# Position bias by w2 times the relu layer in fp32, laid out by DMA, in place of threshold masks

## The chip, the cores and the metric

The kernel runs on one core of one Trainium2 chip. The metric is the device time of one execution in microseconds, the median of three timed runs. The engines are named as the profile names them: PE (TensorE, matrix products) and PEld (its weight loads), DVE (VectorE), ACT (ScalarE), POOL (GpSimd), SP (SyncE, which here only issues DMAs).

## The reference

Attention with a learned position bias, then a gated MLP, then a token and channel mixing stage. All of it is fp32. The part that changes is the bias:

```python
pos = np.arange(S)                       # S = 576
rel = (pos[:, None] - pos[None, :]).astype(np.float32)
psi_rel = np.log1p(np.abs(rel))
psi_i = np.log1p(np.maximum(pos[:, None].astype(np.float32), 1.0))
x = (psi_rel / psi_i)[..., None]
h = np.maximum(x @ w1 + b1, 0.0)         # w1 (1, 32), b1 (32)
bias = h @ w2                            # w2 (32, 8): one bias per head
scores = scores + bias.transpose(2, 0, 1)[None, :, :, :]
...
attn = np.exp(scores)
attn = attn / (np.sum(attn, axis=-1, keepdims=True) + 1e-09)
```

So each pair of a query row i and a key column j has one scalar x, 32 relu units on it, and 8 head biases. The bias is the same for the 4 batches. Shapes: batch 4, 8 heads, 576 positions, head size 64; the later stages are 512 wide (the MLP 1024).

## The kernel before

The bias is made once, at the start, and lies in SBUF for all batches: four tiles `bias0` to `bias3` of 128 query rows x 8 heads x 576 columns, and `biasr`, which holds the last 64 rows with even heads in the lower 64 partitions and odd heads in the upper. Then come 144 attention tiles of 128 rows x 576 columns (16 pairs of heads, 9 tiles each): products `s` from `kh`, `kl` and `qs`; DVE adds the bias and takes the row's extreme in one custom instruction (`e<-s,bias`, which gives the row extreme `m`); ACT takes the exponential; `p` is split into two fp16 halves; a DMA transposes it (`pT`), and PE multiplies with `v` (`px`). Between attention pairs run the MLP of the batch before (`vp`, `up`, `sp`) and, at the start, the unpacking of `w_in` (`rawwi`, `cvawi`). After attention come the output product `op`, the unpacking of further weights (`cvaw_tok`, `wr_w_tok` and the like) and the mixing stages (`tp`, `yp`, `cp`).

The bias before (function `bias_gen`, lines 662 to 773) uses that a relu unit is linear in x on one side of a threshold. 45 units of work, each 128 rows x 64 columns, run through four engines. DVE compares a table of distances `ds` with thresholds `th` and writes a 0/1 mask `mk` of 128 x 2048 fp16, in which the partitions are 4 columns x 32 hidden units. PE takes 16 slices of the mask as weights and multiplies each with `ch` and `cl` (w2 times w1 and w2 times b1 in two fp16 parts), 32 products a unit, into `pb`. This gives slope and offset for each head. ACT copies the offset to `cc`, DVE multiplies the slope with the x table `xt` to `bt` (in every sixth unit ACT copies and POOL multiplies instead), and POOL adds the two into the bias tile. `pb` has two buffers of its own and, for every third unit, one of the score buffers (`PBN`, `pbt`); `mk` has three buffers. Beside it, twelve loads `vr` of v and their squares on ACT give the scale of v.

The order of all instructions is not the order of the code. `Rec` records every operation with a key, and `plan` (line 382) runs a list scheduler over them: each operation has a cost from `cost` (line 549), the key is shifted by a number for each name (`SHIFT`), and where an operation may go to one of several engines (`any`, line 300), a number for each name and engine (`BIAS`) weighs the choice. The instructions are then issued in that order on each engine; each engine and each DMA queue works its own in order. All of them carry the helper's line in the profile (L366), so groups are told apart by tile names.

The last part of a unit, after the products, is:

```python
nc.scalar.activation(cc, pv[:, H:], AF.Copy, scale=ci8)
...
nc.vector.tensor_tensor(tmp[r, :nh], pv[r, hs], xs[r].bc(1, nh), op=ALU.mult)
self.tt(("gpsimd",), dv, tmp[r, :nh], cc[r, hs], ALU.add)
```

Of the kernel before, what the change touches and what calls it, by code (L numbers as in the profile page):

```python
# [218 lines left out]
}  # L219
SHIFT = {  # L220
    "aw": -17.4929, "bias": 41.9326, "biasr": -68.9186, "bsg": 97.9286, "bt": -5.7555, "c": -279.9533, "ca": 22.1144,
    "cc": 295.8081, "ch": -73.6056, "ci": 36.2217, "cl": 17.4554, "cp": 15.2786, "cvaw_ch": 69.6045,
    "cvaw_out": -194.7794, "cvaw_theta": 8.5825, "cvaw_tok": -207.7246, "cvawi": -0.5182, "cvsw_ch": 161.0008,
    "cvsw_out": 0.6877, "cvsw_theta": -99.9127, "cvsw_tok": 85.3798, "cvswi": 2.3671, "ds": 47.8704, "e": -0.6132,
    "eps": 169.8, "fa_c": -50.561, "fa_v": 185.4902, "fa_wi": -255.4938, "fa_ws": 58.9062, "fb_c": -277.5272,
    "fb_v": 19.4726, "fb_wi": -86.0368, "fb_ws": 64.453, "fc_c": 164.9752, "fc_v": 223.2589, "fc_wi": 7.0491,
    "fc_ws": 28.1163, "fd_c": -314.7184, "fd_v": -444.6712, "fd_wi": -6.1476, "fd_ws": -20.5742, "fs_c": 244.1602,
    "fs_v": -273.363, "fs_wi": -108.0749, "fs_ws": -26.7084, "g": 98.9891, "gg": 3.2775, "ghs": -197.3784,
    "gr": 14.9268, "gsc": -167.0231, "gts": 44.5279, "gtu": -15.6392, "gtv": -6.823, "halfpi": 90.4852, "i": 26.7498,
# [351 lines left out]
class K:  # L581
# [74 lines left out]

    def pbt(self, u, n=0):
        if PBN[n % len(PBN)]:
            return self.ps_s.tile([P, 2, 512], F32, tag="sc", bufs=2, name=f"pb{u}")
        return self.ps_b.tile([P, 2, 512], F32, tag="pb", bufs=2, name=f"pb{u}")  # L660

    def bias_gen(self):
# [15 lines left out]
        sg2 = st.tile([P, 1], F32, name="sg2")
        aw = st.tile([P, 1], F32, name="aw")
        rt = st.tile([P, 1], F32, name="rt")  # L680
        nc.vector.tensor_scalar(sg, w1, 0.0, 2.0, op0=ALU.is_ge, op1=ALU.mult)
        nc.vector.tensor_scalar(sg2, sg, -1.0, None, op0=ALU.add)
        nc.vector.tensor_scalar(aw, w1, sg2, 1e-30, op0=ALU.mult, op1=ALU.max)
        nc.vector.reciprocal(rt, aw)
        nc.vector.tensor_scalar(rt, rt, b1, sg2, op0=ALU.mult, op1=ALU.mult)
        nc.vector.tensor_scalar(rt, rt, -1.0, 1e6, op0=ALU.mult, op1=ALU.min)
        nc.vector.tensor_scalar(rt, rt, -1e6, None, op0=ALU.max)
        y, y2 = prow, st.tile([P, S], F32, name="y2")
        nc.vector.tensor_scalar(y, prow, rt, 20.0, op0=ALU.mult, op1=ALU.min)
        nc.vector.tensor_scalar(y, y, -40.0, None, op0=ALU.max)  # L690
        nc.scalar.activation(y2, y, AF.Exp)
        nc.vector.tensor_scalar(y, y2, 700.0, -1.5, op0=ALU.min, op1=ALU.add)
        nc.vector.tensor_scalar(y2, y, MAGIC, MAGIC, op0=ALU.add, op1=ALU.subtract)
        th = st.tile([P, S], F16, name="th")
        self.th = nc.vector.tensor_scalar(th, y2, 0.5, sg2, op0=ALU.add, op1=ALU.mult)
        nc.vector.tensor_scalar(ds, ds, sg2, None, op0=ALU.mult)
        c32 = st.tile([P, 2, H, 4], F32, name="c32")
        nc.vector.memset(c32, 0.0)
        for g in range(4):
            r = slice(32 * g, 32 * g + 32)  # L700
            nc.vector.tensor_scalar(c32[r, 0, :, g], w2[r], w1[r], None, op0=ALU.mult)
            nc.vector.tensor_scalar(c32[r, 1, :, g], w2[r], b1[r], None, op0=ALU.mult)
        c32f = c32.rearrange("p a h g -> p (a h g)")
        junk = self.bsg[:, :64]
        for i in range(2):
            nc.scalar.activation(junk, c32f, AF.Square, accum_out=self.ss_c[:, i:i + 1])
# [634 lines left out]
```

## Time and profile before

| what | us |
|---|---|
| time, median of 3 runs | 963.27 |
| the runs | 957.67, 963.27, 965.01 |
| the profiled execution: span from the first to the last instruction | 948.8 |
| busy PE / PEld | 736.5 / 598.6 |
| busy DVE | 747.9 |
| busy ACT | 562.5 |
| busy POOL | 441.5 |

For the profiled execution the page gives its span and no other time; the median of the runs lies 14.5 us above this span. Busy time is the union of an engine's instructions and says nothing of who waits for whom. That is read from the waits (who waited for whom, and how long) and from the chain that ended last. A mean in nanoseconds is the length of one instruction; instructions of one engine can overlap a little, so a count times a mean can be more than the busy time.

### The profile page before, as it was taken

To read this page: it belongs to the slowest core of one execution; us is meant where nothing else is said; L and a number is where in the kernel's file an instruction comes from. 1 tells how busy PE (TensorE), PEld (TensorE's weight loads), DVE (VectorE), ACT (ScalarE), POOL (GpSimd) and SP (SyncE) were. 2 spreads that over 40 slices of the span, in tenths; PEclk is the share of its full clock that TensorE was granted. 3 is DMA by queue.
4 is the path that set the end of the run, shared out by engine and by line. 5 is a ranking of instruction groups with operands and counts; after the bars stand their busy time and mean duration, and the time that the engine had idled before them with its cause. 6 is when DMAs were issued, how large, how long until landed. Compare 5 with 4: busy or idle time off the path is not lost.

```text
span 948.8 us, 19542 instructions
## 1 busy us (share of the span) xinstructions
PE 736.5 (78%) x7322; PEld 598.6 (63%) x7322; DVE 747.9 (79%) x1544; ACT 562.5 (59%) x1144; POOL 441.5 (47%) x373
## 2 busy tenths in 40 slices
PE   4345445665575895979878989899778999999998
PEld 3345444554464664655555655576757899999998
DVE  8798978889987788998999796898998884372622
ACT  7413148868776777877877684765555673261510
POOL 1667784545545464564556563145643532041310
PEclk9667876756669888899979999999988999999999
DMA  7300019889899999999989995645541110010001
GB/s 250 104 1 2 1 30 255 166 167 217 152 197 207 204 194 183 192 225 218 190 186 199 231 179 154 208 138 176 182 134 48 34 52 34 1 51 1 26 26 50
DMA packets 223871, 124.79 MB, mean 132 GB/s; under 512 B 195616, under 2 KB 195744, under 8 KB 223776
## 3 DMA queue, kind: packets, MB, share of 16 engines
q1 hardware_dynamic: 214560, 101.88, 50.0%
q10 hardware_dynamic: 9216, 21.67, 7.9%
q8 instruction: 57, 0.93, 0.4%
q14 instruction: 38, 0.31, 0.1%
HBM read 62.17 MB, written 14.16 MB: 80 GB/s over the span
## 4 chain that ended last, share of the span: by engine, by line
PE 38%; DVE 28%; DMA 15%; issue 10%; ACT 7%; POOL 1%; SPq 0%; ACTq 0%; DVEq 0%; POOLq 0%
PE yp L366 11%; DMA pT<-p 6%; DVE mk L366 5%; PE cp L366 4%; PE s L366 4%; DVE e L366 4%; PE op L366 3%; PE tp L366 3%; PE pb L366 3%; PE px L366 3%; DMA xp<-x 3%; PE up L366 2%; DVE x L366 2%; DVE cvaw_tok L366 2%; PE sp L366 2%
## 5 line engine op out<-in xcount | busy, mean ns | idle before, releaser
L366 POOL TENSOR_TENSOR p<-e,p 128x576 f16<-128x576 f32 x144 | 194.4, 1358 | 152.7 <-ACT p L366 132.5
L366 PE MATMUL s<-kh,qs 128*128 128x288 f32 (+1 forms) x320 | 94.0, 390 | 63.9 <-DVE m L366 39.6
L366 ACT ACTIVATE e<-e,m 128x576 f32<-128x576 f32 x144 | 110.4, 767 | 42.1 <-DVE m L366 37.7
L366 PE MATMUL px<-v,pT 128*128 128x64 f16 (+1 forms) x2240 | 102.5, 206 | 41.1 <-DMA pT<-p 34.3
L366 PEld LDWEIGHTS <-pT 128*128 128x128 f16 (+1 forms) x2240 | 89.0, 110 | 68.8 <-DMA pT<-p 46.1
L366 PE MATMUL yp<-wk,z 128*128 128x288 f32 x864 | 118.3, 296 | 0.7 <-ACT z L366 0.4
L366 PEld LDWEIGHTS yp<-wk,z 128*128 128x128 f32 x864 | 115.6, 188 | 1.8 <-ACT z L366 0.9
L366 PEld LDWEIGHTS s<-kh,qs 128*128 128x128 f32 (+1 forms) x320 | 59.3, 222 | 85.5 <-DVE m L366 31.7
L366 PE MATMUL pb<-ch,mk 128*128 128x64 f16 x720 | 60.0, 213 | 65.6 <-ACT cc L366 34.4
L366 DVE CUSTOM_DVE_ANT_0 e<-s,bias 128x576 f32<-128x576 f32 x128 | 95.7, 751 | 13.0 <-PE s L366 11.4
L366 ACT ACTIVATE p<-e 128x576 f16<-128x576 f32 x140 | 92.8, 671 | 18.3 <-DMA pT<-p 13.5
L366 PEld LDWEIGHTS <-mk 128*128 128x128 f16 x1440 | 58.4, 111 | 68.0 <-DVE mk L366 54.8
L366 PE MATMUL s<-kl,qs 128*128 128x288 f32 (+1 forms) x320 | 84.9, 362 | 6.4 <-DVE kl L366 6.1
L366 DVE TENSOR_TENSOR mk<-ds,th 128x2048 f16<-128x2048 f16 x45 | 79.5, 1817 | 5.2 <-PE pb L366 5.1
L366 POOL TENSOR_TENSOR bias<-bt,cc 128x512 f32<-128x512 f32 x36 | 62.1, 1745 | 42.8 <-ACT cc L366 24.0
L366 PE MATMUL op<-sp_g,wo 128*128 128x288 f32 x384 | 65.0, 328 | 14.6 <-DVE x L366 9.3
L366 PEld LDWEIGHTS op<-sp_g,wo 128*128 128x128 f32 x384 | 59.1, 212 | 21.3 <-DVE x L366 7.0
L366 PEld LDWEIGHTS s<-kl,qs 128*128 128x128 f32 (+1 forms) x320 | 62.1, 228 | 10.2 <-DVE kl L366 9.2
L366 ACT ACTIVATE cc<-pb,ci 128x512 f32<-128x512 f32 x45 | 29.6, 683 | 62.5 <-DVE bt L366 56.7
L366 PE MATMUL vp<-wi,xT 128*128 128x512 f16 (+1 forms) x240 | 64.2, 395 | 2.2 <-DVE gg L366 2.2
L366 PE MATMUL sp<-ws,n 128*128 128x64 f16 (+1 forms) x384 | 58.7, 293 | 2.8 <-DVE n L366 2.7
L366 DVE TENSOR_TENSOR x<-x,yp 128x576 f32<-128x576 f32 x16 | 12.1, 754 | 61.6 <-PE yp L366 61.6
(228 smaller groups left out, 1651.5 us busy)
## 6 DMA issues: line engine op xcount, KB each, us to landing
raw<-kv ACTq DMA_DIRECT2D x19, 576.0 KB, 4.9
raw<-kv SPq DMA_DIRECT2D x13, 576.0 KB, 4.7
raww_tok<-w_tok SPq DMA_DIRECT2D x18, 288.0 KB, 3.0
vr<-v_all SPq DMA_DIRECT2D x12, 384.0 KB, 3.8
xx<-dx SPq DMA_DIRECT2D x16, 288.0 KB, 3.2
out<-oo SPq DMA_DIRECT2D x16, 288.0 KB, 2.1
xT<-dx SPq DMA_DIRECT2D x7, 576.0 KB, 5.2
gr<-dg SPq DMA_DIRECT2D x14, 288.0 KB, 3.3
```

The lines of the kernel that those rows point to most:

```text
L366: getattr(getattr(self.nc, name), m)(*[res(x) for x in a], **out)
```

## The change

The bias is computed as the reference writes it, in fp32. The partitions are now 4 query rows x 32 hidden units. A table `lt` holds log1p of the distance for a window of 1148 positions, shifted by one from one row of the four to the next, and `sl` holds w1 divided by psi of each row. For four rows at a time one instruction makes the relu layer `hq` (128 x 576): on DVE as max(lt * sl, -b1) with the constant part w2 times b1 added later (`cb`), and, in every third group, on ACT as relu(lt * sl + b1). 144 of these make 36 groups `G` of four. For each group PE multiplies each of the four `hq` with the same small weights `w2f` (128 x 32) in two halves of 288 columns; the four results go to the four 32-partition column groups of one `pb` tile. So a group has 8 products, 288 in all. One instruction (ACT or DVE, as the planner chooses) copies the 128 x 576 result to `bs`, whose partitions are row and head, and a DMA lays it out as 16 rows x 8 heads x 576 in the bias tile. There are no masks, no `xt`, no `bt`, no `cc`, and no POOL work for the bias. `pb` uses its own two buffers alone. `hq` has ten buffers, `bs` three. `cost` prices a product with 32 output partitions at a quarter. The tables of the planner have other numbers throughout, and the DMA issues have numbers of their own in them now.

```diff
 BIAS = {
-    ("gg", "gpsimd"): -9.3524, ("gg", "vector"): -1.4198, ("kh", "scalar"): -12.8265, ("kh", "vector"): 14.8773,
...
+    ("bias", "scalar"): -23.814, ("bias", "sync"): 24.2122, ("biasr", "scalar"): -42.8956,
...
-        return rhs.cols * (4.0 if rhs.t.dt == F32 else 1.068 if rhs.t.dt == F32R else 1.0), rhs.shape[0] / P
+        n = rhs.cols * (4.0 if rhs.t.dt == F32 else 1.068 if rhs.t.dt == F32R else 1.0)
+        return (n / 4 if out.shape[0] == 32 else n), rhs.shape[0] / P
...
-TWO = range(4,45,6)
-PBN = (0,0,1)
+LUTG = 3
...
-        for x, n in ((wb, "wb"), (prow, "prow"), (ds, "dtab")):
-            self.ld(x, d[n], ("sync",))
-        for ib in range(5):
-            nc.key = 1.0 + 15 * ib
-            self.ld(xt[:, ib], d["xtab"][:, ib], ("sync",))
...
+        sl = st.tile([P, S // 4], F32, name="sl")
+        lt = st.tile([P, DW], F32, name="lt")
+        for x, n in ((wb, "wb"), (sl, "rpsi"), (lt, "ltab")):
+            self.ld(x, d[n])
+        nb = st.tile([P, 1], F32, name="nb")
+        nc.vector.tensor_scalar(nb, b1, -1.0, None, op0=ALU.mult)
+        self.th = nc.vector.tensor_scalar(sl, sl, w1, None, op0=ALU.mult)
...
-        for n in range(45):
-            nc.key = 2.0 * n
-            ib, js = divmod(n, 9)
...
-                nc.vector.tensor_tensor(mk, win, th[:, ib * P:(ib + 1) * P].bc(1, 16), op=ALU.is_gt)
...
-            for J in range(16):
-                o = ps[:, J // 8].rearrange("p (r j) -> p r j", j=32)[:, :, J % 8 * 4:J % 8 * 4 + 4]
-                nc.tensor.matmul(o, mk[:, J, :], chv, start=True, stop=False)
-                nc.tensor.matmul(o, mk[:, J, :], clv, start=False, stop=True)
...
+        for g in range(4):
+            nc.tensor.matmul(pc[32 * g:32 * g + 32, 0:1], w2f, bb, start=True, stop=True)
+        nc.vector.tensor_copy(cb, pc[:, 0:1])
...
+        for G in range(36):
+            ps = self.ps_b.tile([P, 2, 512], F32, tag="pb", bufs=2, name=f"pb{G}")
+            hs = []
+            lut = G % LUTG == LUTG - 1
+            for q in range(4):
+                nc.key = 2.5 * G + q * 0.5
+                Q = 4 * G + q
+                h = st.tile([P, S], F32, tag="hq", bufs=10, name=f"hq{Q}")
+                win = lt[:, DOFF - 4 * Q:DOFF - 4 * Q + S]
+                if lut:
+                    nc.scalar.activation(h, win, AF.Relu, scale=sl[:, Q:Q + 1], bias=b1)
+                else:
+                    nc.vector.tensor_scalar(h, win, sl[:, Q:Q + 1], nb, op0=ALU.mult, op1=ALU.max)
+                hs.append(h)
+            for n in range(2):
+                for q in range(4):
+                    nc.tensor.matmul(ps[32 * q:32 * q + 32, n, :SH], w2f, hs[q][:, n * SH:(n + 1) * SH],
+                                     start=True, stop=True)
+            bs = st.tile([P, S], F32, tag="bs", bufs=3, name=f"bs{G}")
+            bv = bs.rearrange("p (n j) -> p n j", n=2)
+            add = zero if lut else cb
+            nc.any(("scalar", "activation", (bv, ps[:, :, :SH], AF.Identity), {"bias": add}),
+                   ("vector", "tensor_scalar", (bv, ps[:, :, :SH], add, None), {"op0": ALU.add}))
+            ib, r0 = divmod(16 * G, P)
...
+                self.ld(self.bm[ib][r0:r0 + 16], bs)
...
+                for e in range(2):
+                    self.ld(self.bm[4][64 * e + r0:64 * e + r0 + 16], bs[e::2])
```

DVE in the middle of the bias, before: masks `mk` (block and unit in the name), and between them the multiplications `bt`.

```order
L366 TENSOR_TENSOR mk1_3_735<-ds_199,th_192 128x2048
L366 TENSOR_TENSOR bt1_2_787<-pb1_2_655,xt_198 128x512 [waits Activation_49]
L366 TENSOR_TENSOR mk1_4_774<-ds_199,th_192 128x2048
L366 TENSOR_TENSOR mk1_7_865<-ds_199,th_192 128x2048 [waits DVE_49,PE_49]
L366 TENSOR_TENSOR mk1_8_902<-ds_199,th_192 128x2048 [waits DVE_49,PE_49]
L366 TENSOR_TENSOR bt1_3_897<-pb1_3_776,xt_198 128x512 [waits Activation_49]
L366 TENSOR_TENSOR bt1_4_908<-pb1_4_790,xt_198 128x512 [waits Pool_49]
L366 TENSOR_TENSOR bt1_5_932<-pb1_5_746,xt_198 128x512 [waits Pool_49]
L366 TENSOR_TENSOR mk2_0_960<-ds_199,th_192 128x2048 [waits DVE_49,PE_49]
L366 TENSOR_TENSOR bt1_6_962<-pb1_6_906,xt_198 128x512 [waits Activation_49]
```

DVE at the fifth to eighth group, after: the relu rows `hq` (numbered by four rows) and the copies `bs` (numbered by group); `kl` belongs to attention.

```order
L379 TENSOR_SCALAR hq16_268<-lt_189,sl_190,nb_188 128x576 [waits DVE_49,PE_49]
L379 TENSOR_SCALAR hq17_276<-lt_189,sl_190,nb_188 128x576 [waits DVE_49,PE_49]
L379 TENSOR_SCALAR bs2_173<-pb2_259,zb_184 128x576 [waits PE_49]
L379 TENSOR_SCALAR bs3_271<-pb3_285,cb_185 128x576 [waits DMAHW3_49,PE_49,Activation_49]
L379 TENSOR_SCALAR hq18_283<-lt_189,sl_190,nb_188 128x576
L379 TENSOR_SCALAR hq19_288<-lt_189,sl_190,nb_188 128x576 [waits Activation_49]
L379 TENSOR_TENSOR kl0_0_111<-raw0_0_118,kh0_0_114 128x576 [waits DMAHW1_49,Activation_49]
L379 TENSOR_SCALAR hq24_312<-lt_189,sl_190,nb_188 128x576 [waits DVE_49]
L379 TENSOR_SCALAR hq27_326<-lt_189,sl_190,nb_188 128x576 [waits DVE_49,PE_49]
L379 TENSOR_SCALAR hq28_337<-lt_189,sl_190,nb_188 128x576 [waits PE_49,Activation_49]
L379 TENSOR_SCALAR hq29_343<-lt_189,sl_190,nb_188 128x576 [waits DVE_49,PE_49]
L379 TENSOR_SCALAR bs5_324<-pb5_318,zb_184 128x576 [waits DMAHW7_49,PE_49]
```

The masks and multiplications are gone; relu rows stand in their place, with a copy `bs` now and then that waits for the products of its group and, from the fourth on, for a DMA as well, because its buffer must have been laid out.

The SP queue around the third to sixth `vr` load, before:

```order
L366 DMA xt_198<-xtab 128x576 [waits DMAHW4_49]
L366 DMA vr2_251<-v_all 128x768 [waits DMAHW6_49,Activation_49]
L366 DMA vr3_265<-v_all 128x768 [waits DMAHW7_49,Activation_49]
L366 DMA rq0_0_117<-qt 64x576 [waits DMAHW0_49]
L366 DMA vr4_333<-v_all 128x768 [waits DMAHW1_49,Activation_49]
L366 DMA vr5_360<-v_all 128x768 [waits DMAHW2_49,Activation_49]
L366 DMA vr6_446<-v_all 128x768 [waits DMAHW3_49,Activation_49]
```

The same place after; `bias0<-bs` is the layout of one group, 16 rows x 8 heads x 576:

```order
L379 DMA vr2_249<-v_all 128x768 [waits DMAHW2_49,Activation_49]
L379 DMA bias0_78<-bs0_171 16x8x576 [waits DMAHW3_49,Activation_49]
L379 DMA vr3_266<-v_all 128x768 [waits DMAHW4_49,Activation_49]
L379 DMA bias0_78<-bs1_172 16x8x576 [waits DMAHW5_49,Activation_49]
L379 DMA vr4_304<-v_all 128x768 [waits DMAHW6_49,Activation_49]
L379 DMA bias0_78<-bs2_173 16x8x576 [waits DMAHW7_49,DVE_49]
L379 DMA bias0_78<-bs3_271 16x8x576 [waits DMAHW0_49,DVE_49]
L379 DMA vr5_347<-v_all 128x768 [waits DMAHW1_49,Activation_49]
L379 DMA bias0_78<-bs4_298 16x8x576 [waits DMAHW2_49,Activation_49]
L379 DMA vr6_367<-v_all 128x768 [waits DMAHW3_49,Activation_49]
L379 DMA bias0_78<-bs5_324 16x8x576 [waits DMAHW4_49,DVE_49]
L379 DMA bias0_78<-bs6_332 16x8x576 [waits DMAHW5_49,Activation_49]
```

Between the loads `vr` stand the layout DMAs, each behind its copy on ACT or DVE, and the loads behind them wait in the queue. Of the 40 layout DMAs (32 of 16x8x576, 8 of 16x4x576) 38 are on SP and two, those of group 34, on ACT.

PE from the fifth group on, after; the column group is the number of `hq` modulo four:

```order
L379 MATMUL pb4_310<-hq16_268,w2s_187 32x288
L379 MATMUL pb4_310<-hq17_276,w2s_187 32x288
L379 MATMUL pb4_310<-hq16_268,w2s_187 32x288
L379 MATMUL pb4_310<-hq17_276,w2s_187 32x288
L379 MATMUL pb5_318<-hq20_291,w2s_187 32x288 x2
L379 MATMUL pb4_310<-hq18_283,w2s_187 32x288 x2
L379 MATMUL pb5_318<-hq21_293,w2s_187 32x288 x2
L379 MATMUL pb4_310<-hq19_288,w2s_187 32x288 x2
L379 MATMUL pb5_318<-hq22_306,w2s_187 32x288 x2
L379 MATMUL pb6_354<-hq24_312,w2s_187 32x288
L379 MATMUL pb6_354<-hq25_314,w2s_187 32x288
L379 MATMUL pb6_354<-hq24_312,w2s_187 32x288
```

The planner has mixed two groups and split some pairs of halves; where a row ends in x2, both halves of one column group follow each other directly.

## Rows read from the trace of the kernel before

**Rows 1.** Windows, four stretches: busy us (instructions), granted clock, DMA share, GB/s.
```profile
10.00:132.00 122.00, 61.09 (x1443) 58.79 (x1444) 107.32 (x94) 44.56 (x76) 79.94 (x52) 0.78 0.15 49
145.00:580.00 435.00, 329.23 (x3509) 238.48 (x3509) 383.17 (x982) 334.21 (x715) 232.31 (x198) 0.83 0.98 194
580.00:750.00 170.00, 148.44 (x987) 111.76 (x985) 144.26 (x267) 98.84 (x203) 75.06 (x72) 0.95 0.45 141
750.00:949.00 199.00, 194.04 (x1363) 186.84 (x1361) 97.98 (x145) 72.18 (x125) 44.91 (x37) 1.00 0.09 31
```

**Rows 2.** Lines, 10 to 132 us: count | busy us, mean ns | idle before, releasers.
```profile
L366 DVE TENSOR_TENSOR mk<-ds,th 128x2048 f16<-128x2048 f16 x45 | 79.5, 1817 | 5.2 <-PE pb L366 5.1
L366 POOL TENSOR_TENSOR bias<-bt,cc 128x512 f32<-128x512 f32 x36 | 62.1, 1745 | 42.8 <-ACT cc L366 24.0 <-DVE bt L366 18.5
L366 PE MATMUL pb<-ch,mk 128*128 128x64 f16 x720 | 60.0, 213 | 65.6 <-ACT cc L366 34.4 <-DVE mk L366 27.4 <-DVE bt L366 3.8
L366 DVE TENSOR_TENSOR bt<-pb,xt 128x512 f32<-128x512 f32 (+1 forms) x42 | 24.6, 608 | 6.3 <-POOL bias L366 3.5 <-ACT cc L366 1.9 <-POOL biasr L366 0.5
```

**Rows 3.** Waits, 10 to 135 us: us in total, times, longest.
```profile
PEld L366 <- DVE mk L366: 54.8, 25, 6.8
```

**Rows 4.** Timeline: start us, us, what; first masks, first attention tile, last bias add.
```profile
10.74 4.63 DVE L366 TENSOR_TENSOR mk<-ds,th 128x2048 f16<-128x2048 f16 x4
...
132.39 0.76 DVE L366 CUSTOM_DVE_ANT_0 e<-s,bias 128x576 f32<-128x576 f32 x1 [0.46 <-PE s L366]
...
137.77 3.77 POOL L366 TENSOR_TENSOR biasr<-bt,cc 64x256 f32<-64x256 f32 x5
```

**Rows 5.** Lines by form, whole span, VectorE: count | busy us, mean ns | idle.
```profile
L366 DVE TENSOR_TENSOR x<-x,yp 128x576 f32<-128x576 f32 x16 | 12.1, 754 | 61.6 <-PE yp L366 61.6
L366 DVE TENSOR_SCALAR prow<-prow,rt 128x576 f32<-128x576 f32 x1 | 0.5, 520 | 0.0
L366 DVE TENSOR_SCALAR y<-prow 128x576 f32<-128x576 f32 x1 | 0.5, 461 | 0.0
```

**Rows 6.** Lines by form, whole span, ScalarE.
```profile
L366 ACT ACTIVATE kh<-raw 128x576 fp32r<-128x576 f32 x32 | 21.5, 673 | 9.7 <-DMA raw<-kv 7.9 <-DMA xp<-x 1.5
L366 ACT ACTIVATE v<-raw,fc_v 128x576 f16<-128x576 f32 x25 | 19.2, 768 | 5.9 <-PE px L366 3.9 <-DMA xp<-x 1.2 <-DVE fc_v L366 0.7
L366 ACT ACTIVATE vr<-vr 128x768 f32<-128x768 f32 x12 | 10.1, 842 | 7.1 <-DMA vr<-v_all 7.0
```

**Rows 7.** Lines by form, whole span, TensorE.
```profile
L366 PE MATMUL yp<-wk,z 128*128 128x288 f32 x864 | 118.3, 296 | 0.7 <-ACT z L366 0.4 <-DVE x L366 0.3
L366 PE MATMUL xp<-ident,x 128*128 128x128 f32 x64 | 10.0, 278 | 3.9 <-DVE rk L366 2.6 <-DVE rw L366 1.3
L366 PE MATMUL pbv<-ssv,ones 128*128 128x2 f32 x2 | 0.4, 262 | 0.4 <-ACT cc L366 0.4
```

**Rows 8.** DMA issues, whole span: KB each, median us to landing.
```profile
rq<-qt SPq DMA_DIRECT2D x20, 144.0 KB, 2.9
wb<-wb SPq DMA_DIRECT2D x1, 5.0 KB, 1.6
```

**Rows 9.** DMA, 0 to 36 us, 40 slices of 0.9 us.
```profile
GB/s 0 1 50 287 396 389 255 300 376 407 404 407 373 411 420 409 329 56 73 273 137 283 126 0 109 300 147 256 89 174 271 156 140 304 201 212 17 0 0 61
```

**Rows 10.** Lines by form, 130 to 949 us: work that changes its engine.
```profile
L366 POOL TENSOR_TENSOR wk<-wr_w_tok,wk 128x576 fp32r<-128x576 f32 x9 | 13.8, 1532 | 9.3 <-ACT wk L366 9.3
L366 POOL TENSOR_TENSOR wr_w_ch<-cvaw_ch,cvsw_ch 128x256 f32<-128x256 f32 x8 | 6.3, 787 | 8.4 <-ACT cvaw_ch L366 7.6 <-ACT cvsw_ch L366 0.9
L366 DVE CAST x<-xf 128x256 f16<-128x256 f32 x7 | 3.5, 498 | 1.2 <-DMA xp<-x 1.1
L366 DVE TENSOR_TENSOR wr_w_theta<-cvaw_theta,cvsw_theta 128x256 f32<-128x256 f32 x2 | 1.8, 908 | 0.0
```

**Rows 11.** Chain that ended last, 150 to 580 us, by line.
```profile
by line: DMA pT<-p 14.2%; PE s L366 9.2%; issue 8.9%; DVE e L366 7.8%; PE px L366 6.1%; DMA xp<-x 5.5%; DMA rawwi<-w_in 3.8%; DVE x L366 3.6%; PE vp L366 2.6%; ACT e L366 2.6%; DVE cvawi L366 2.5%; DMA raw<-kv 2.5%; DVE gtv L366 2.4%; DVE k
```

More of the change, by code (lines that the diff above doesn't have):

```diff
@@ new lines @@
+    ("biasr", "sync"): -32.2509, ("bs", "scalar"): -0.0729, ("bs", "vector"): 0.2057,
+    ("bsg", "scalar"): -10.0381, ("bsg", "sync"): -2.7396, ("g", "scalar"): 10.6989, ("g", "sync"): 44.9021,
+    ("gg", "gpsimd"): 0.6847, ("gg", "scalar"): 4.2248, ("gg", "sync"): -24.7139, ("gg", "vector"): 26.751,
+    ("gr", "scalar"): -0.003, ("gr", "sync"): 40.0654, ("ident", "scalar"): -56.6989,
+    ("ident", "sync"): -54.8165, ("kh", "scalar"): -16.1883, ("kh", "vector"): -12.6842,
[4 rows of a table added]
+    ("qs", "vector"): 0.9315, ("raw", "scalar"): -8.224, ("raw", "sync"): 3.4229, ("raww_ch", "scalar"): 4.5613,
@@ L219 @@
+    ("wr_w_tok", "gpsimd"): 29.6991, ("wr_w_tok", "vector"): 23.1577, ("ws", "scalar"): -11.5258,
+    ("ws", "vector"): 61.9014, ("wsr", "scalar"): 11.35, ("wsr", "vector"): -19.7126,
[4 rows of a table added]
 }
 SHIFT = {
-    "aw": -17.4929, "bias": 41.9326, "biasr": -68.9186, "bsg": 97.9286, "bt": -5.7555, "c": -279.9533, "ca": 22.1144,
-    "cc": 295.8081, "ch": -73.6056, "ci": 36.2217, "cl": 17.4554, "cp": 15.2786, "cvaw_ch": 69.6045,
-    "cvaw_out": -194.7794, "cvaw_theta": 8.5825, "cvaw_tok": -207.7246, "cvawi": -0.5182, "cvsw_ch": 161.0008,
@@ L224 @@
[L224 to L228, printed above, removed]
@@ L241 @@
-    "xr": 152.077, "xs": -346.0698, "xt": 28.8733, "xx": -162.3402, "y": -5.0366, "yp": 12.4507, "z": -39.0017,
-}
-LOADF, LOADK = 0.8525, 326.367
-BV = 0.5800719398726655
+    "": 64.6628, "bb": 172.4547, "bias": -15.0872, "biasr": -3.9853, "bs": -109.3335, "bsg": 191.2664,
+    "cb": 127.7869, "cp": 27.5766, "cvaw_ch": 82.2283, "cvaw_out": -229.6304, "cvaw_theta": -77.909,
+    "cvaw_tok": -146.3463, "cvawi": 1.3215, "cvsw_ch": 15.8659, "cvsw_out": 36.3779, "cvsw_theta": -243.4725,
+    "cvsw_tok": -6.4709, "cvswi": 1.4061, "e": -0.6863, "eps": -47.8983, "fa_v": 228.9712, "fa_wi": -446.4475,
@@ L245 @@
+    "wr_w_ch": 93.529, "wr_w_out": 114.2337, "wr_w_theta": 7.4639, "wr_w_tok": -29.2476, "ws": 18.8185,
+    "wsr": -346.125, "wt": 522.892, "x": -6.1563, "xT": 323.1668, "xf": 3.3878, "xfr": -9.808, "xp": 39.5334,
+    "xr": 126.5857, "xs": -750.4002, "xx": -204.6706, "yp": 25.4727, "z": -144.0222, "zb": 15.8229,
+}
+LOADF, LOADK = 0.6551125965057019, 140.07673330286215
+BV = 0.3058631898588213
 TABLES = {AF.Exp: 0, AF.Tanh: 0, AF.Gelu_apprx_tanh: 1, AF.Sin: 2}
-SLACK = 0.5924
+SLACK = 1.0108193382555337
@@ L678, in bias_gen @@
[L678 to L698, printed above, removed]
+        sl = st.tile([P, S // 4], F32, name="sl")
[4 more added lines that the diff above has]
+        nc.vector.tensor_scalar(nb, b1, -1.0, None, op0=ALU.mult)
@@ L699, in bias_gen @@
+        self.th = nc.vector.tensor_scalar(sl, sl, w1, None, op0=ALU.mult)
+        w2s = st.tile([P, 4, H], F32, name="w2s")
+        nc.vector.memset(w2s, 0.0)
         for g in range(4):
             r = slice(32 * g, 32 * g + 32)
[L701 to L706, printed above, removed]
@@ L707, in bias_gen @@
-        cs, ci = self.pow2(self.pbt("c")[:, 0], self.ss_c, 2, "c")
-        ci8 = st.tile([P, 1], F32, name="ci8")
-        nc.vector.tensor_scalar(ci8, ci[:, 0:1], 8.0, None, op0=ALU.mult)
-        ch = st.tile([P, 64], F16, name="ch")
-        cl = st.tile([P, 64], F16, name="cl")
-        nc.vector.tensor_scalar(ch, c32f, cs[:, 0:1], None, op0=ALU.mult)
-        nc.vector.scalar_tensor_tensor(cl, c32f, cs[:, 0:1], ch, op0=ALU.mult, op1=ALU.subtract)
-        chv, clv = (x.rearrange("p (r g) -> p r g", g=4) for x in (ch, cl))
@@ L716, in bias_gen @@
[L716 to L723 removed]
+            nc.vector.tensor_scalar(w2s[r, g], w2[r], 8.0, None, op0=ALU.mult)
@@ new lines, in bias_gen @@
+        w2f = w2s.rearrange("p g h -> p (g h)")
+        cb = st.tile([P, 1], F32, name="cb")
+        bb = st.tile([P, 1], F32, name="bb")
+        pc = self.ps_b.tile([P, 2, 512], F32, tag="pb", bufs=2, name="pbc")[:, 0]
+        nc.vector.tensor_copy(bb, b1)
+        for g in range(4):
+            nc.tensor.matmul(pc[32 * g:32 * g + 32, 0:1], w2f, bb, start=True, stop=True)
+        nc.vector.tensor_copy(cb, pc[:, 0:1])
+        zero = st.tile([P, 1], F32, name="zb")
+        nc.vector.memset(zero, 0.0)
@@ L744, in bias_gen @@
-            tmp = st.tile([P, H, 2, 32], F32, tag="bt", bufs=3, name=f"bt{ib}_{js}")
-            two = n in TWO
-            cc = st.tile([P, H, 2, 32], F32, tag="cc", bufs=3, name=f"cc{ib}_{js}")
-            nc.scalar.activation(cc, pv[:, H:], AF.Copy, scale=ci8)
-            if two:
-                ca = st.tile([P, H, 2, 32], F32, tag="ca", bufs=2, name=f"ca{ib}_{js}")
-                nc.scalar.activation(ca, pv[:, :H], AF.Copy)
-            for r, hs, nh, dst in parts:
-                dv = dst[r, :, js * 64:(js + 1) * 64].rearrange("p h (k j) -> p h k j", k=2)
-                if two:
-                    nc.gpsimd.tensor_tensor(tmp[r, :nh], ca[r, hs], xs[r].bc(1, nh), op=ALU.mult)
-                else:
-                    nc.vector.tensor_tensor(tmp[r, :nh], pv[r, hs], xs[r].bc(1, nh), op=ALU.mult)
-                self.tt(("gpsimd",), dv, tmp[r, :nh], cc[r, hs], ALU.add)
+                self.ld(self.bm[ib][r0:r0 + 16], bs)
+            else:
+                for e in range(2):
+                    self.ld(self.bm[4][64 * e + r0:64 * e + r0 + 16], bs[e::2])
@@ L770, in bias_gen @@
         nc.vector.tensor_reduce(ssv[:, 1:2], self.ss_v, mybir.AxisListType.X, ALU.add)
-        sc, iv = self.pow2(self.pbt("v")[:, 0], ssv, 2, "v")
+        sc, iv = self.pow2(self.ps_b.tile([P, 2, 512], F32, tag="pb", bufs=2, name="pbv")[:, 0], ssv, 2, "v")
         self.sv, self.iv = sc[:, 0:1], iv[:, 0:1]
@@ L1296, in layout @@
     a["wb"] = np.tile(w, (4, 1))
-    pos = np.arange(S)
-    pi = np.log1p(np.maximum(pos.astype(f), f(1.0)))
-    a["prow"] = np.tile(pi[None], (P, 1))
-    a["dtab"] = np.abs(np.arange(DW)[None] - DOFF - (np.arange(P) // HID)[:, None]).astype(np.float16)
-    rel = np.log1p(np.abs((pos[:, None] - pos[None]).astype(f)))
-    x = (rel / pi[:, None]).astype(f)
-    x = np.concatenate([x, x[512:]], axis=0)
-    a["xtab"] = x.reshape(5, P, S).transpose(1, 0, 2)
+    psi = np.log1p(np.maximum(np.arange(S).astype(f), f(1.0)))
+    a["rpsi"] = np.repeat((f(1.0) / psi).reshape(S // 4, 4).T, HID, axis=0)
+    a["ltab"] = np.log1p(np.abs(np.arange(DW)[None] - DOFF - (np.arange(P) // HID)[:, None]).astype(f))
     a["ident"] = np.eye(P, dtype=f)
```

49 lines of the change are left out of this document (11 added, 38 removed), and 40 rows, old and new, of tables (BIAS, SHIFT).

## The prediction

> **What bounds the kernel now.** I read the windows first. From 10 to 132 us only the bias is made: DVE is busy 107.3 of 122 us, POOL 79.9, PE 61.1, ACT 44.6 [rows 1]. The groups of that stretch say with what: 45 masks of 1.82 us are 79.5 us, the multiplications `bt` 24.6, while PE's weight loads wait 54.8 us for masks and the masks wait only 5.1 us for PE [rows 2, 3]. So the bias phase is a DVE phase. The timeline gives its ends: the first mask starts at 10.7 us, the last bias addition ends at 137.77 + 3.77 = 141.5 us, and the first attention tile is at 132.4 [rows 4]. From there to 580 us DVE is still at 383 of 435 us and the DMA engines at 0.98, and the chain names DVE and DMA lines in turn [rows 1, 11]; from 750 us on PE is busy 194 of 199 us [rows 1]. The change can therefore gain as many microseconds as the bias phase gets shorter, if the order behind it stays as good.
>
> Does attention move into the bias phase? The order says no. Its first tile stands behind the 30th of 36 copies on DVE, and there are two tiles ahead of the last group, as before there were two ahead of the last addition. So I move the end of the bias phase and let the rest follow.
>
> **What goes.** 45 masks, 30 + 16 `bt`, all POOL work on the bias, 1440 products, `cc`: nothing of it remains to hide behind something else. POOL's 80 us [rows 1] are worth nothing by themselves, since they lie beside the DVE work.
>
> **What comes, as four streams that run side by side from about 7 us** (the threshold computation is gone, so the first relu row waits for the 588 KB of `lt` alone, 1.5 us at the 400 GB/s that loads over 128 partitions reach [rows 9], behind a first landing at about 2.4 us [rows 8]).
>
> DVE: 96 relu rows with two pointer operands. 461 ns without one and 520 with one [rows 5] make 579 with two; 96 x 0.579 = 55.6. 15 copies at 0.754 [rows 5] are 11.3, `kl` and `qs` 1.8: 68.7 us.
>
> ACT: 48 relu rows. 673 ns without a pointer and 768 with one [rows 6] make 863; 41.4 us. 21 copies at 0.77 are 16.2, twelve `vr` at 0.84 are 10.1 [rows 6]: 67.7 us. DVE and ACT are level, 1.9 us a group each.
>
> PE: no row shows an fp32 product of 288 columns or products in separate column groups. From below: one fp32 product appears as two records (`pbv`) [rows 7], each at least one pass like `yp`, 118.3 / 864 = 0.137 us, so 0.27. From above: the fp32 transposes cost 10.0 / 64 = 0.156 us for 128 columns, 2.6 times `yp` per column, so 2 x 0.35 = 0.70. I take the middle, 0.48. All 288 one behind the other are 138 us, all perfectly four abreast 35; these are the ends of this term. In the order as written the two records of a product and often both its halves use the same column group in a row. Following the 576 records through it, each starting when its predecessor has started and its own column group is free, gives 84 us at the full clock, 2.3 us a group, and 165 us at half of it.
>
> DMA: 40 layout transfers, 36 times 295 KB, each written to 16 partitions. No row shows this. From below: 400 GB/s [rows 9], 0.74 us each. From above: if the rate falls with the partitions written, 16 of 128 give 50 GB/s, 5.9 us. The nearest row is `rq`, 64 partitions: 144 KB land after 2.9 us, 5 KB after 1.6 [rows 8], so 1.3 us more for 139 KB. I take that rate, the row with the fewest partitions: 2.6 us each, 36 x 2.6 = 94. In the same queue stand nine more `vr` (393 KB, 1 us each) and 2 us for the first heads: 105 us. This stream starts at about 11.5 us, after the first group, and its last landing takes 2 us. With 5% lost between waits: 11.5 + 105 / 0.95 + 2 = 124 us. PE gives 7 + 84 + 5 = 96, DVE and ACT about 80. The layout transfers end last.
>
> [...]
>
> New waits: from the fourth group on a copy `bs` waits for the layout three groups before. Behind it on DVE or ACT are queued the next relu rows, for which PE waits. The SP queue waits for the copies, and behind each layout stand `vr` loads for which ACT's squares wait. This couples the streams; the 5% is for that.
>
> End of the bias phase 141.5 to 124: **-17.5 us.**
>
> **Behind it.** The refitted order gives DVE work that others had: 25 casts of `x` at 0.50, 16 small ones at 0.3, nine `wk` at about 0.75, 14 `wr` at 0.91 [rows 10], less four `wt` of 1.0: 36 us with the small ones. POOL loses 28 us of that (nine at 1.53, eight at 0.79 and six alike [rows 10]), ACT 18. At its worst all 36 are on the path; at best DVE finds POOL in its way less often and 10 us are gained (a `wr` of 256 columns took 0.91 us on DVE and 0.79 on POOL, so DVE was held up). The DVE lines named in the chain add up to 16% [rows 11]; I take a sixth of 36, **+6 us**. The cover that ended is POOL's and ACT's idle time, in which this work lay before.
>
> **Sum.** 948.8 - 17.5 + 6 = 937.3 us of span. The runs' median lies 14.5 us above the span of the profiled execution, which I carry over: **951.8 us**, 1.2% faster.
>
> **Rivals.** The time is 963.3 - 141.5 + 6 + the end of the bias phase.
> - The layout is a little slower, 2.65 to 3.15 us a transfer. At 2.8, 36 x 2.8 + 11 = 112, end 11.5 + 112 / 0.95 + 2 = 131, time 959: no change. For it: `rq` writes to four times as many partitions, and nothing in the trace writes to so few; the layout is the one stream with an unseen price. Against: DMA engines that stood at a share of 0.15 in this stretch [rows 1] have room. **Above 3.15 us it is slower** (end 145, time 973), with 5.9 us far outside (1076).
> - PE takes over as the bound and is slower than DVE was. If the column groups do not overlap, 288 x 0.48 = 138 us at the full clock, end 150 with 7 us of start and 5 of tail, time 978. It is slower from 133 us of PE work on, which half the clock gives too (165 us, end 177, 1005). For it: in the bias phase the granted clock was 0.78 with PE half busy, and 1.00 only where PE is always busy [rows 1], and the order runs one column group twice in a row. Against: a PE that is the bound is always busy, and so gets the full clock as in the last stretch.
> - The layouts are cheap, 0.74 to 2.2 us, and PE ends the phase: 84 / 0.95 + 12 = 100, time 928.
>
> **How the numbers follow.** A measurement tells about 1% from no change here, 9.6 us: faster means under 953.6, slower over 972.9. The likeliest is the forecast, layouts of 2.2 to 2.65 us (936 to 953): 0.30, of it 0.27 faster, 0.03 same. Cheap layouts 0.18, faster. Layouts of 2.65 to 3.15 us 0.22, of it 0.02 faster, 0.20 same. Layouts above that 0.12, slower. PE as the bound 0.18, of it 0.14 slower, 0.03 same, 0.01 faster. That is 0.48 faster, 0.26 same, 0.26 slower. The range runs from 908 (PE ends the phase at 96 without loss, and 10 us are gained behind it) to 985 (layouts of 3.5 us, end 158; or PE serial with 5% lost): what it leaves out is half the clock, and layouts slower still. The forecast's own range, with the term behind it uncertain by 10 us, is 930 to 965.
>
> **What would show it.** Right: the first relu row at about 7 us, copies `bs` 3 us apart on average, the last layout landing near 124 us, waits of `bs` for "bias" DMAs, PE pieces of 288 columns overlapping in time, DVE and ACT 60% busy there. Layouts that follow one another in much less or more than 2.6 us would prove the DMA term wrong; PE without waits and matmuls end to end in that stretch, the PE term; a stretch from the end of the bias phase to the end that is not 948.8 - 141.5 + 6 = 813 us, within 10 us, the term behind. It is wrong as a whole if the last layout lands after 136 us.

## The result and the profile after

The changed kernel takes 927.21 us (median of 4 runs, 916.49 to 935.06); the kernel before, with one more run beside it, 963.09. The ratio is 0.961, with a 95% interval of 0.953 to 0.968: 3.9% faster. The slowest of the four, 935.06 us, counts as a slow execution, and the ratio leaves it out. Forecast were 951.8 us, a range of 908 to 985, and faster as the likeliest. The profiled execution took 916.49 us for a span of 914.7; its span is 34.1 us shorter than before's. Each profile shows one execution that is shorter than its kernel's median (the medians are 35.9 us apart), and all that follows on where the time went is read from these two.

The windows, cut near the end of the bias and at the third attention tile (as in [rows 1]: busy us, granted clock, DMA share, GB/s; a share above 1 means that packets of one DMA engine overlap in time):

```profile
10.00:115.00 105.00, 68.64 (x564) 27.48 (x559) 62.28 (x125) 62.97 (x97) 4.24 (x3) 0.87 0.99 146
115.00:126.00 11.00, 2.81 (x21) 2.46 (x22) 2.99 (x7) 2.55 (x7) 0.00 (x0) 0.50 1.14 219
126.00:537.00 411.00, 319.30 (x3386) 233.40 (x3385) 379.83 (x1008) 313.02 (x656) 229.29 (x182) 0.83 0.99 198
537.00:697.00 160.00, 140.23 (x1000) 104.41 (x1001) 135.65 (x281) 91.87 (x193) 59.57 (x60) 0.92 0.56 162
697.00:914.00 217.00, 211.03 (x1467) 202.34 (x1465) 110.66 (x173) 83.18 (x147) 48.48 (x36) 0.99 0.08 29
```

In the bias phase no engine is full, but the DMA engines are: their share was 0.15 before [rows 1] and is 0.99 now, at 146 GB/s, where loads over 128 partitions reached 400 and more [rows 9]. The groups of this stretch answer to [rows 2]:

```profile
L379 PE MATMUL pb<-hq,w2s 128*32 128x288 f32 x576 | 70.7, 474 | 31.4 <-DVE bs L379 15.2 <-ACT bs L379 13.0 <-DVE hq L379 2.6
L379 DVE TENSOR_SCALAR hq<-lt,sl,nb 128x576 f32<-128x576 f32 x96 | 48.9, 574 | 5.3 <-PE pb L379 3.7 <-DMA lt<-ltab 1.4
L379 ACT ACTIVATE hq<-lt,wb,sl 128x576 f32<-128x576 f32 x48 | 38.9, 855 | 3.0 <-DMA lt<-ltab 3.0
...
L379 ACT ACTIVATE bs<-pb,cb 128x576 f32<-128x576 f32 x16 | 11.8, 740 | 32.3 <-PE pb L379 14.5 <-DMA bias<-bs 14.4 <-DVE hq L379 3.3
...
L379 DVE TENSOR_SCALAR bs<-pb,cb 128x576 f32<-128x576 f32 x8 | 6.5, 818 | 10.8 <-DMA bias<-bs 8.7 <-PE pb L379 2.0
```

PE waits for copies `bs`, and the copies wait for layouts that hold their buffers. That is the chain of a phase paced by its DMAs: 38.5 us of such waits in all (5 to 112 us; engine that waits, for what, total, times, longest):

```profile
DVE bs L379 <- DMA bias<-bs: 24.1, 11, 6.5
...
ACT bs L379 <- DMA bias<-bs: 14.4, 6, 3.6
```

The DMA issues of the page (KB each, median us from issue to landing), and then GB/s in 40 slices of the stretch 82 to 110 us, in which nearly only layouts run:

```profile
bias<-bs SPq DMA_DIRECT2D x32, 288.0 KB, 7.1
...
vr<-v_all SPq DMA_DIRECT2D x12, 384.0 KB, 8.6
...
biasr<-bs SPq DMA_DIRECT2D x6, 144.0 KB, 4.9
```

```profile
GB/s 109 132 109 114 99 158 105 105 109 168 151 109 112 109 151 105 109 145 105 120 105 148 119 105 171 201 125 105 125 148 109 105 158 82 174 175 79 16 89 184
```

105 to 109 GB/s is the floor to which the row returns: one layout alone. The lower values near the end are DMA engines without work. These are the stretches of the phase in which the share is full or falls:

```profile
10.60:68.00 57.40, 38.51 (x309) 15.47 (x308) 34.40 (x63) 33.73 (x54) 0.00 (x0) 0.88 1.03 164
68.00:70.50 2.50, 1.53 (x16) 0.67 (x18) 0.72 (x3) 2.32 (x5) 0.00 (x0) 0.50 0.28 56
70.50:105.00 34.50, 25.58 (x227) 10.27 (x222) 22.76 (x45) 24.03 (x34) 1.80 (x2) 0.93 1.04 125
105.00:110.50 5.50, 2.41 (x18) 0.90 (x12) 3.79 (x13) 1.42 (x2) 1.16 (x1) 0.88 0.59 125
```

The timeline gives the phase's ends: first relu rows and products, the last layouts, and the third attention tile, before (the first line) and after.

```profile
146.36 0.76 DVE L366 CUSTOM_DVE_ANT_0 e<-s,bias 128x576 f32<-128x576 f32 x1 [0.94 <-PE s L366]
```

```profile
5.53 1.56 DVE L379 TENSOR_SCALAR hq<-lt,sl,nb 128x576 f32<-128x576 f32 x3 [1.39 <-DMA lt<-ltab]
...
6.16 1.18 PE L379 MATMUL pb<-hq,w2s 128*32 128x288 f32 x3 [2.58 <-DVE hq L379]
...
109.20 1.20 SPq L379 DMA_DIRECT2D biasr<-bs  x2
...
110.50 7.75 SPq L379 DMA_TRANSPOSE pT<-p  x2
...
114.74 8.50 ACTq L379 DMA_DIRECT2D rs<-w_sg  x5
118.31 0.52 DVE L379 TENSOR_SCALAR v<-raw,fc_v 128x576 f16<-128x576 f32 x1 [8.24 <-DMA raw<-kv]
...
123.29 0.68 ACT L379 ACTIVATE kh<-raw 128x576 fp32r<-128x576 f32 x1 [11.89 <-DMA rawwi<-w_in]
...
125.70 0.76 DVE L379 CUSTOM_DVE_ANT_0 e<-s,bias 128x576 f32<-128x576 f32 x1
```

The last layout is issued by 110.4 us and lands at 116.0 (before, the last addition ended at 141.5 [rows 4]): **-25.5 us.** Then the third attention tile comes 9.7 us later and not 4.9. Its load, two transposes and five loads `rs` now meet DMA engines that are still full of layouts, and then of each other; before, the share of the DMA engines had been 0.22 until then. These are the windows (before, then after) and the five `rs` issues (ns of one, then start of the first and the last):

```profile
128.00:142.00 14.00, 4.71 (x88) 4.04 (x88) 10.74 (x24) 5.77 (x10) 12.82 (x16) 0.76 0.22 41
```

```profile
110.50:123.30 12.80, 0.36 (x7) 0.37 (x8) 1.07 (x2) 0.88 (x4) 1.27 (x1) 0.50 1.11 162
```

```profile
L379 ACTq DMA_DIRECT2D rs<-w_sg x5: 335/460/541, 114.7 to 122.9; - x5
```

An issue takes 0.3 to 0.5 us. The five stretch over 8.5 us because each waits until the DMA that last used its landing semaphore has landed (the `DMAHW` waits in the order): the third for `raw` (118.3 us), the fifth for the first transpose, which lands 12.4 us after its issue at 110.5, against 3.3 us for one before. ACT works its queue in order, so `kh`, and with it the third tile, comes behind the fifth, at 123.3 us. **+4.8.** From the third tile to the end it is 914.7 - 125.7 = 789.0 us, before 948.8 - 146.4 = 802.4: **-13.4** (by the medians of the runs, 35.9 - 20.7 = 15.2). The three add up to the 34.1.

### The profile page after: what moved, and what is told of

Same layout as the page of the kernel before. It is cut to its first block, busy times and chain, and to the rows that moved or that the text cites. A ratio compares the mean times of both kernels' runs of the same rounds, so it can differ in the third digit from the quotient of the medians.

```text
span 914.7 us, 17891 instructions
## 1 busy us (share of the span) xinstructions
PE 746.1 (82%) x6464; PEld 572.0 (63%) x6464; DVE 697.4 (76%) x1614; ACT 558.8 (61%) x1106; POOL 341.8 (37%) x283
## 4 chain that ended last, share of the span: by engine, by line
PE 41%; DVE 27%; DMA 19%; issue 5%; ACT 5%; SPq 1%; POOL 1%; ACTq 0%; DVEq 0%; POOLq 0%
PE yp L379 12%; DMA bias<-bs 8%; PE cp L379 5%; DVE e L379 5%; PE s L379 4%; PE tp L379 4%; DMA pT<-p 4%; DVE x L379 3%; PE px L379 3%; PE op L379 3%; PE vp L379 3%; PE sp L379 2%; PE up L379 2%; PE pb L379 2%; DVE cvawi L379 2%
## 5 line engine op out<-in xcount | busy, mean ns | idle before, releaser
L379 POOL TENSOR_TENSOR p<-e,p 128x576 f16<-128x576 f32 x144 | 199.6, 1398 | 155.9 <-ACT p L379 101.1
L379 PE MATMUL px<-v,pT 128*128 128x64 f16 (+1 forms) x2240 | 104.4, 208 | 41.7 <-DMA pT<-p 37.9
L379 PE MATMUL pb<-hq,w2s 128*32 128x288 f32 x576 | 70.7, 474 | 31.4 <-DVE bs L379 15.2
L379 ACT ACTIVATE p<-e 128x576 f16<-128x576 f32 x136 | 88.8, 671 | 11.7 <-DMA pT<-p 11.1
L379 PEld LDWEIGHTS pb<-hq,w2s 128*32 128x32 f32 x576 | 27.7, 121 | 72.3 <-ACT bs L379 22.2
L379 PE MATMUL vp<-wi,xT 128*128 128x512 f16 (+1 forms) x240 | 62.2, 388 | 2.7 <-DMA xT<-dx 2.1
L379 ACT ACTIVATE sp_u<-x 128x576 fp32r<-128x576 f32 x16 | 11.0, 685 | 82.3 <-DVE x L379 82.1
L379 POOL TENSOR_TENSOR z<-rr,z 128x512 fp32r<-128x512 f32 x16 | 22.6, 1415 | 92.8 <-ACT z L379 92.8
L379 PE MATMUL up<-xT,wi 128*128 128x64 f16 (+1 forms) x384 | 56.0, 289 | 0.3 <-DVE gtv L379 0.2
```

The source lines that it names most:

```text
L379: getattr(getattr(self.nc, name), m)(*[res(x) for x in a], **out)
```

## Experiments

In "order held" kernels the planner's order of the changed kernel is replayed instruction by instruction, so that nothing moves but the edit. The planner's answer to any edit would otherwise reshuffle all that follows. The kernels ran at different times, so they are compared by their ratio to the kernel before, run beside each; the changed kernel's is 0.961 (0.953 to 0.968). The expected times count from its 927 us; beside these runs the kernel before took 956.6 to 961.5 us and not 963.1, so where time and ratio differ, the ratio decides. Times per packet are means over the DMA records of one size in the bias phase: 2304 B for the layouts (and a few `rq`), 3072 B for `vr`.

**The layout over all partitions.**

```diff
-                self.ld(self.bm[ib][r0:r0 + 16], bs)
+                self.ld(self.bm[ib][:, G % 8], bs)
```

> The order of all instructions is held exactly as in the changed kernel; only the 32 layouts of 16 x 8 x 576 write the same 295 KB, in the same 128 packets of 2304 B, to all 128 partitions (one head slot of the bias tile) instead of 16. The bias then holds the wrong rows. Theory P (a layout is dear because it writes to 16 partitions only): a packet falls from 266 ns on average to 93 to 125 ns, the layouts no longer fill the DMA engines (share in the bias phase from 0.97 to 0.5 to 0.6), the last biasr issue moves from 110 us to 95 to 102, and the time from 927 to 912 to 919. Theory V (the DMA engines are full by volume, or the phase is paced by copies and products anyway): packets stay above 200 ns, or they fall and the phase still ends at 107 to 110 us; time 923 to 930.

Measured: 889.43 us, ratio 0.927 (0.919 to 0.935). A packet took 111 ns (266 in the changed kernel), the copies' waits for layouts all but vanished, the last layout was issued by 77.6 us, and the third tile began at 92.1. In the stretch 10 to 79 us (the line of the windows, then the products, then the layouts with their time to landing):

```profile
10.00:79.00 69.00, 59.06 (x561) 28.02 (x558) 62.88 (x125) 62.10 (x97) 3.20 (x3) 0.99 0.69 214
```

```profile
L379 PE MATMUL pb<-hq,w2s 128*32 128x288 f32 x576 | 61.2, 420 | 8.9 <-DVE bs L379 3.4 <-ACT bs L379 2.6 <-DVE hq L379 2.4
```

```profile
bias<-bs SPq DMA_DIRECT2D x32, 288.0 KB, 3.0
```

P holds and V falls, but the gain was over twice what P said: with cheap layouts PE, DVE and ACT are level at 59 to 63 us of 69, so the phase could end 17 to 24 us earlier than the 95 to 102 I had allowed. The write to 16 partitions costs the changed kernel some 34 us at the third tile. The wait behind the last issue stays: 14.6 us to the third tile here, 15.3 in the changed kernel.

**Which partitions.** The same 16 rows, but on every eighth partition, with the order held; the query rows are dealt out in the host's layout.

```diff
-                self.ld(self.bm[ib][r0:r0 + 16], bs)
+                self.ld(self.bm[ib][G % 8::8], bs)
...
+    dealt = np.arange(512).reshape(4, 8, 16).transpose(0, 2, 1).reshape(-1)
-    qt = np.concatenate([qt[..., 512:], qt[..., :512]], axis=3)
+    qt = np.concatenate([qt[..., 512:], qt[..., :512][..., dealt]], axis=3)
```

> The order is held as in the changed kernel. The 16 rows of a group go to every eighth partition of the bias tile (8r + g) instead of 16 neighbours, and the query rows are dealt out in the same way in the host's layout of q, w_sg, b_sg, w_tok and of the output, so the whole computation is the same. [...] Rival C (what counts is the number of partitions, 16 as before): packets and time as in the changed kernel, 922 to 930.

Measured: 903.12 us, ratio 0.942 (0.935 to 0.950): faster than both kernels. A packet took 164 ns on average. In the stretch with nearly only layouts its median was 179 ns (60 to 82 us), against 314 in the changed kernel (82 to 108 us), where that of a layout by itself is 354. C falls: the number of partitions is 16 in both, so it counts which ones are written; why is not shown. I had expected 890 to 900 us, near the 889 of the write to all partitions, and missed it by 3. The last layout is issued by 84.3 us, 26 earlier than in the changed kernel, and the third tile starts at 101.2; from there to the end it takes 800.6 us, 11.6 more than in the changed kernel. But the changed kernel's profile is of its fastest execution, 10.7 us under its median, so a loss behind the phase is not shown. The bias phase (windows, 10 to 88 us):

```profile
10.00:88.00 78.00, 60.19 (x564) 27.50 (x559) 62.97 (x124) 62.52 (x97) 4.10 (x3) 0.98 0.83 195
```

**Two queues.** Layouts of odd groups on ACT's queue.

```diff
-                self.ld(self.bm[ib][r0:r0 + 16], bs)
+                self.ld(self.bm[ib][r0:r0 + 16], bs, (("sync",), ("scalar",))[G % 2])
```

> Layouts of even groups on the SP queue, of odd groups on the ACT queue, so that two neighbours, which write to different 16 partitions, can be under way together. Theory P: mean packet of a layout from 266 ns to 180 to 220, last biasr issue at 100 to 106 us instead of 110, time 915 to 923. Theory V, or ACT held up at its issues by as much as the layouts gain: time 925 to 937.

Measured: 951.09 us, ratio 0.988 (0.981 to 0.994). A miss for P's numbers, and slower than V allowed too: a packet took 273 ns, as with one queue, and the last layout was issued by 118 us. A second queue did not make a layout cheaper. That the phase ended later is not the layouts' doing alone, since the DMA engines had gaps (a share of 0.84 from 82 to 110 us, against 1.05 from 82 to 105 in the changed kernel). Here the order was not held, and most of the loss lies behind the phase (815.9 us from the third tile), as in the other kernels below whose order the planner made anew.

**More buffers for the copies.** `bufs=3` of `bs` becomes 5, order held.

> The order held as in the changed kernel, five bs buffers instead of three. Theory P (the layouts end last and pace the phase; waits of copies for them are a consequence): fewer waits of bs for bias DMAs, the last biasr issue within 3 us of 110, time 922 to 931. Rival (the coupling, copies that wait for a buffer and stop the relu rows behind them, costs time by itself): the phase ends at 104 or before, time under 921.

Measured: 915.07 us, ratio 0.959 (0.951 to 0.966), the same as the changed kernel. The copies' waits fell from 38.5 to 7.5 us and the last layout was issued at 109.2 instead of 110.4, so these waits only showed who is late. The third tile starts at 118.4 us, 7.3 earlier; the time does not show it, but 7 us are within the two intervals. The waits:

```profile
DVE bs L379 <- DMA bias<-bs: 5.1, 2, 4.1
...
ACT bs L379 <- DMA bias<-bs: 2.4, 2, 1.4
```

The same on top of the dealt rows:

> The rows dealt out to every eighth partition, and five bs buffers, the order held: the whole computation is the same. [...]

Measured: 895.79 us, ratio 0.942 (0.935 to 0.949), the ratio of the dealt rows with three buffers; no difference is shown.

**DVE's 36 us.** The order held, but 41 copies of `x`, nine `wk`, 14 `wr` and four `wt` on the engines that had them before.

In short, names and engines with their counts:

```diff
-('x', 'vector') x41  ('wk', 'vector') x9  ('wr_w_ch', 'vector') x8  ('wr_w_theta', 'vector') x6  ('wt', 'gpsimd') x4
+('x', 'scalar') x41  ('wk', 'gpsimd') x9  ('wr_w_ch', 'gpsimd') x8  ('wr_w_theta', 'gpsimd') x6  ('wt', 'vector') x4
```

> The order held as in the changed kernel, but 41 copies of x go back to ACT, nine wk, eight wr_w_ch and six wr_w_theta back to POOL, and four wt back to DVE, as before: the 36 us of work that the refit gave DVE. My prediction's term (a sixth of it, 6 us, lies on the path): time 915 to 924. If DVE's extra work costs nothing where it lies: 924 to 931. Rival L (POOL in DVE's way and POOL's slower instructions cost more): 932 or more, with the loss behind 560 us, where wk and wr are.

Measured: 920.61 us, ratio 0.968 (0.960 to 0.975), which overlaps that of the changed kernel. In the profiled executions the stretch from the third tile to the end is 918.2 - 129.3 = 788.9 us, against 789.0. So no cost of this work on DVE is shown. My 6 us would have made the ratio about 0.955, under this interval, and the loss that L expects does not lie where L placed it.

**Is it the numbers, or the fit?** First each kernel with the other's numbers for all names outside the bias (`BIAS`, `SHIFT` and the planner's constants):

> The changed code, with the planner's numbers of before for every name outside the bias (and its load, slack and yield constants). Theory R (what was gained behind the bias phase is the refitted order): the bias phase ends within 5 us of where it does now, the stretch from there to the end grows by 10 to 16 us, time 937 to 945. Theory N (the gain behind comes with the bias phase itself, an idle POOL and earlier loads): the stretch grows by less than 4 us, time 924 to 931.

> The kernel before, with the refitted numbers for every name outside the bias. Theory R, if the numbers are good by themselves: 10 to 16 us less behind the bias phase, time 947 to 954. Theory N: within 4 us of 963. If the numbers only fit the code they were fitted to: slower than 967, which says nothing against R.

Measured: the changed code with the old numbers 948.54 us, ratio 0.988 (0.980 to 0.996); the kernel before with the new numbers 970.59, ratio 1.008 (1.004 to 1.013). Each is worse off with the numbers of the other. The first lost more than R said; the second is slower than 967, the case in which the new numbers only fit the code they were fitted to and are not better by themselves. Then each kernel's own numbers were shaken a little (two seeds; the kernels hold the resulting numbers):

```diff
-SHIFT = {n: v, ...}
+SHIFT = {n: v + r.gauss(0, 0.5), ...}
```

> The changed code with its own tables, each number of SHIFT moved by a random amount of about 0.5 (normal, one seed); engine choices keep their numbers. Theory F (the gain behind the bias phase is the fit of the order to this very program, so any other order loses it): time 938 to 955, the bias phase ends within 6 us of where it does, the loss lies in the attention stretch and the one behind it. Theory R (it comes from what the numbers say, as more work on DVE): time 922 to 932, since the numbers say nearly the same.

> The kernel before with the same kind of jitter on its own SHIFT. Theory F: its order too was a fit to its program, so it loses as well, 970 to 985. If it loses clearly less than the changed kernel does, the refit of the changed kernel was the better one by the difference. Theory R: 958 to 967.

> The changed code with its own tables, SHIFT moved by about 0.5 with another seed. Theory F (fit): 938 to 955 again, as with the first seed (946). If it is near 927, the first seed was an accident and the order carries no fit worth the name.

> The kernel before with the second seed. Theory F: 970 to 992 again. If the two programs lose alike, this and the run beside it stand apart by what the two fitted kernels stand apart, 3 to 5%, and the gain behind the bias phase does not come from a better fit. If the changed kernel's unfitted orders stand at the same distance only by the bias phase (27 us of 970, 2.8%), the rest was fit.

| profiled execution | ratio, 95% interval | third tile starts | from there to the end |
|---|---|---|---|
| before / changed | 1 / 0.961 | 146.4 / 125.7 | 802.4 / 789.0 |
| before shaken, seed 1, 2 | 1.031 (1.021 to 1.041), 1.021 (1.014 to 1.027) | 146.3, 145.4 | 833.3, 820.4 |
| before, new numbers | 1.008 | 147.2 | 816.5 |
| changed shaken, seed 1, 2 | 0.989 (0.983 to 0.996), 1.014 (1.006 to 1.022) | 124.8, 125.5 | 819.8, 836.2 |
| changed, old numbers | 0.988 | 128.8 | 828.5 |
| changed, two queues | 0.988 | 131.6 | 815.9 |

The third column is steady within 4 us but for the two queues: the bias phase hardly depends on the order. The last one is not. Noise of 0.5 in the planner's numbers costs either kernel 18 to 47 us behind the bias phase. Orders that nobody fitted take 816 to 833 us before (mean of three 823) and 816 to 836 after (mean of four 825). Each is one execution, and executions of one kernel differ by 13 us here (960.3 to 973.9 for the kernel before with the new numbers); that of the old numbers is the slowest of its four, by 10 us. F holds, with more loss for the second seed than I said. By the means the unfitted kernels differ by little more than the bias phase: the shaken ones' ratios, 1.026 and 1.002, stand 2.4% apart, and the 20.7 us up to the third tile are 2.1% of 963. That speaks for a better fit as the source of the 13.4 us, and not better numbers or engines. But by seed they stand 4.2% and 0.7% apart, and the fitted ones 3.9%: the source is not settled.

## Why the prediction was right, and where it was not

- **What bounds:** right. DVE gave up the phase and the layouts took it, as forecast; copies waited for "bias" DMAs, and no rival took its place. PE did not become the bound, although the rival in which it does names 928 us: that agreement is chance.
- **DVE and ACT:** right. Relu rows were forecast at 579 and 863 ns and took 574 and 855; copies at 0.754 and 0.77 us took 0.82 and 0.74.
- **PE:** the product was right, the stream too long. At the full clock (granted 1.00 from 75 to 105 us) the pieces start either about 243 ns after the one before, which I read as the same column group, or mostly 6 to 7 ns after it, as another: 0.486 us a product against 0.48. So by this reading column groups do overlap; a piece does not carry its group in the profile, so no view here shows their order. The count of 84 us rested on a rule for the starts that was my estimate, shown by no row; with cheap layouts PE was busy for 61 us. Often four pieces start within 20 ns, and the next four 243 ns later (85.51, 85.78, 86.02 and 86.26 us in the changed kernel), where the count had two pieces of one product in a row. This term was not on the path.
- **The layout's price:** 2.6 us was right in sum and wrong in kind, and that is luck. (By the row it came from it should have been 2.7: 1.3 us for 139 KB, and a layout is 288 in the same unit.) A layout that runs alone has packets of 354 ns: 2304 B x 16 engines / 354 ns = 104 GB/s, or 128 x 0.354 / 16 = 2.83 us. That is the 2.8 us by which I had called no change, a price that no row of before shows. The dealt rows, on as many partitions but every eighth, took 179 ns a packet at the median, with nearly only layouts under way: the price hangs on which partitions are written. Beside other transfers a layout's packets took 266 ns on average, 2.13 us a layout. The `vr` loads between them paid for it, with 264 ns a packet against 159 before: 2.1 us each and not 1.0. So the layouts took 77 us and not 94, the `vr` loads took more than forecast, and all packets of the phase sum to 104 us of the 16 engines, against 105 forecast.
- **The step that failed first: "with 5% lost between waits" and 2 us of tail.** The stream started at 10.6 us (11.5 forecast) and ended at 116.0, not 124: 8 us. It lasted 105.4 us for 104 us of packets. The DMA engines did stand, at 68 to 70.5 us (share 0.28) and from 105 to 110.5 (0.59); but elsewhere their packets overlap to a share of 1.03 to 1.04, which makes up for it. A layout lands 7.1 us after its issue while the next follows 2.8 us later, so two or three are under way, and most waits of a copy cost the DMA engines nothing.
- **The step that failed second: "behind it, +6 us".** I forecast 813 us, within 10, from the end of the bias to the end, and it was 914.7 - 116.0 = 798.7. The mechanism I priced, a sixth of DVE's 36 us on the path, does not show (and the work listed there adds up to 33, not 36). What I had not priced are +4.8 us of loads that pile up where the DMA engines used to be idle, and -13.4 us behind the third tile, for which a better fit of the order is likely and not shown: 14.6 us of error against the 813.3 of my sum.
- **The carry-over:** the median lay 12.5 us above the span of the profiled execution, against 14.5: 2 us. The three errors make the 24.6 us between 951.8 and 927.2.

The forecast's own range, 930 to 965, missed by 3 us; the wide one held.

## What to carry to other kernels

Price a DMA by where it writes, not by its bytes. This planner counted 0.82 us for a layout (295 KB at its 360 GB/s) that took 2.1 to 2.8, and dealing the same rows out to every eighth partition brought 2% more, with only the host's layout changed. When an order has been fitted by search, do not price the stages behind the change from the instructions that were moved: shake the order of both kernels, and take the distance between the unfitted ones as what the change does by itself, with more seeds than the two here, which gave 4.2% and 0.7%. A wait with a long total names the late party only; here the copies' waits fell by 31 us and the time stayed.
